# RWKV recurrence and gated feed-forward on one core: START worked out anew, VectorE's and GpSimd's shares exchanged

## The chip, the cores and the metric

One core of a Trainium2 chip. Five engines work side by side: TensorE (matmul and weight load), VectorE, ScalarE, GpSimd and SyncE, which issues most DMAs. The metric is the device time of one execution in microseconds; lower is better. SBUF is the on-chip memory of 128 partitions, PSUM the accumulator memory that TensorE writes. GpSimd's operands here all lie in SBUF.

## What is computed

A linear recurrence over 768 steps for 4 sequences of 8 heads with 48 channels, and on its result a feed-forward layer of 384 to 1536 to 384 channels for all 3072 tokens:

```
for t in range(S):                                   # r, k, v: (4, 8, 768, 48); w, u: (8, 48)
    cur = einsum('bhd,bhe->bhde', u[None] * kt, vt)
    y[:, :, t] = einsum('bhd,bhde->bhe', rt, state + cur)
    state = w[None, :, :, None] * state + einsum('bhd,bhe->bhde', kt, vt)
x = y as (3072, 384)
out = (1 / (1 + exp(-(x @ w_gate))) * (x @ w_val)) @ w_out
```

## The kernel before, in words

**Attention.** The steps are cut into 12 chunks of 64 tokens, and each chunk into two groups of heads: 24 groups, GROUPS[n] = (chunk, half), the half with index 1 first. For one group: loads of the channel layout (L, 512 KB) and the token layout (X, 400 KB); VectorE or GpSimd multiplies queries (R or Rv, line 303), keys (k, line 309) and token keys (T or Tv, line 313) by powers of w; ScalarE makes the keys with u (A, line 282); TensorE makes the 64 x 64 scores (Z, line 350); VectorE copies them through the masks into a score tile (K, line 364); TensorE applies state and scores (I: from_state, then the scores times v) and makes the outer products of the state's update (O, line 405, through into_y at line 322). ScalarE decays the state (d), VectorE adds to it (s; for chunk 0 a copy, sa, on ScalarE). The result y goes from PSUM to x as a rounded high part (h, ScalarE, line 458) and the low rest (l, VectorE, line 462). Channels of the fourth head pair are moved into free partitions of the other three by small DMAs (fills: F, line 466).

**Feed-forward.** x comes in tiles of two chunks, 512 columns. A matmul is done as three passes over high and low parts, low weights first. The hidden channels lie in 12 blocks f. Per block: 18 matmuls up into two PSUM banks (U, line 499), sigmoid of one (g, ScalarE, line 508), product (m, VectorE, line 512), high part (H, ScalarE, line 517), low part (q on GpSimd, qv on VectorE, line 521), 9 matmuls down into three accumulators (D, line 537). For tile 0 blocks 0 and 1 are done for each chunk by itself, with 256 columns: items 0 and 1 are chunk 0, items 2 and 3 chunk 1; items 4 to 13 are blocks 2 to 11 with 512.

**Weights** arrive as 64-bit floats, 1152 KB a block (W, line 232), and are turned into two 32-bit parts in the kernel: ScalarE scales the upper words (c, line 238), VectorE joins (j: three operations, lines 244 to 246), ScalarE rounds the high part (w, line 252), GpSimd (o) or VectorE (ov) takes the low part (line 255). Block 0 is done in halves (c0, j0, w0, o0, o0v).

**Order.** Nothing is scheduled by the compiler: every engine runs its instructions in the order in which the code issues them. START is a list of steps, written out, that covers the attention of chunks 0 to 3 (groups 0 to 7) and the whole feed-forward of tile 0 with the weights of all blocks; the number behind the dot is the group, the block (W, c, j, w, o) or the item (U, g, m, H, q, D). After it a regular loop does tiles 1 to 5 with attention in fixed slots. What sets the order around START is, besides that list, which buffers are free: three of `chan`, three of `toks`, two of `dec`, and three PSUM banks called `ring`, of which each U and each I takes two. A step that finds its buffer in use waits, and with it all that is queued behind it on its engine, SyncE's DMAs too. Other names in START: tk, ti, tp are VectorE's tables of powers, tc constants (GpSimd) with ScalarE's table load, tt a turn of the table on TensorE, tn its copy by ScalarE.

Of the kernel before, what the change touches and what calls it, by code (L numbers as in the profile page):

```python
# [17 lines left out]
B, H, S, D = 4, 8, 768, 48  # L18
# [6 lines left out]
CT = B * C  # L25
# [13 lines left out]


START = """
tk ti tp L.0 Rv.0 W.0 tc A.0 k.0 c0.0 tt L.1 c0.1 X.0 Z.0 j0.0 tn K.0 X.3 I.0 A.1 Tv.0 w0.0 X.1 h.0
k.1 R.1 Z.1 j0.1 l.0 L.2 R.2 K.1 A.2 L.3 k.2 O.0 sa.0 T.1 w0.1 I.1 h.1 Rv.3 W.1 l.1 c.1 Z.2 K.2 L.4
o0.1 O.1 sa.1 o0.0 j.1 F.0 U.0 A.3 W.2 X.2 k.3 g.0 w.1 I.2 m.0 H.0 Tv.2 O.2 ov.1 d.2 X.7 R.4 h.2 s.2
l.2 A.4 Z.3 U.1 K.3 k.4 g.1 T.3 L.5 m.1 c.2 I.3 j.2 d.3 O.3 Z.4 h.3 H.1 W.4 q.0 X.4 D.0 w.2 l.3 s.3
W.7 F.2 c.4 K.4 W.3 U.2 g.2 q.1 A.5 m.2 Rv.5 k.5 T.4 U.3 g.3 L.6 X.5 o.2 j.4 I.4 d.4 H.2 O.4 Z.5 D.1
s.4 q.2 X.6 h.4 W.5 W.6 m.3 l.4 D.2 Tv.5 c.3 j.3 w.4 A.6 H.3 U.4 K.5 g.4 w.3 I.5 m.4 L.7 ov.3 q.3 O.5
d.5 W.10 R.6 h.5 H.4 ov.4 l.5 s.5 q.4 c.5 D.3 k.6 c.6 U.5 g.5 D.4 A.7 W.9 W.8 j.5 w.5 m.5 H.5 U.6 j.6
w.6 k.7 g.6 q.5 D.5 ov.5 Z.6 m.6 U.7 ov.6 c.8 H.6 c.7 K.6 g.7 q.6 Tv.6 I.6 O.6 Rv.7 Z.7 m.7 H.7 D.6
d.6 q.7 D.7 j.7 h.6 w.7 l.6 s.6 ov.7 j.8 U.8 g.8 w.8 m.8 K.7 H.8 qv.8 ov.8 c.9 U.9 g.9 c.10 j.9 D.8  # L50
m.9 U.10 w.9 F.6 ov.9 g.10 m.10 H.9 I.7 H.10 qv.9 qv.10 W.11 c.11 d.7 T.7 O.7 D.9 j.10 h.7 w.10 s.7
l.7 D.10 ov.10 j.11 U.11 g.11 m.11 H.11 qv.11 U.12 w.11 ov.11 D.11 g.12 m.12 F.7 H.12 qv.12 U.13 g.13
D.12 m.13 H.13 q.13
"""


# [1 line left out]
def rwkv_then_moe(ctx: ExitStack, tc: tile.TileContext, wd, ch, tk, rt, ut, wt, rk0, vn0, wd0, out):  # L58
    nc = tc.nc
# [21 lines left out]
    def one_bank():  # L81
        return ring.tile([P, 512], F32, name="ring")
# [12 lines left out]
    w = wu[:, 0]  # L95
# [162 lines left out]
    xt, dec, ga, yb, kv = {}, {}, {}, {}, {}  # L258
# [135 lines left out]

    def outer(n, banks=None):
        k, v = toks[n][:, 0], toks[n][:, 1]
        if banks is not None:
            kv[n] = banks
        for p, p2 in PP:
            for be in range(2):  # L400
                for gm in range(2):
                    row, at = slice(64 * gm, 64 * gm + 64), (4 * p + 2 * (be ^ gm) + p2) * D
                    m, o = D if be else 64, 256 + (2 * p + p2) * D
                    if banks is not None:
                        nc.tensor.matmul(  # L405
                            banks[64 * be : 64 * be + m, gm ^ be, o - 256 : o - 256 + D],
                            k[row, at : at + m], v[row, at : at + D], start=True, stop=True,
                        )
# [20 lines left out]
    def add_state(n, copy=nc.vector.tensor_copy):  # L429
        g, st = states(n)  # L430
        for s in range(2):
            y = (kv[n][:, s, 0 : 4 * D] if n in kv else yb[n][s][:, 256 : 256 + 4 * D])[0:112]
            y = y.rearrange("q (p x) -> q p x", p=2)
            if GROUPS[n][0]:
                nc.vector.tensor_tensor(st[:, :, s], st[:, :, s], y, ALU.add)
            else:
                copy(out=st[:, :, s], in_=y)
# [105 lines left out]
    def accumulators():  # L543
        return [pacc.tile([P, 512], F32, name=f"acc{d}") for d in range(3)]
# [77 lines left out]
    n = FIRST  # L622
# [51 lines left out]
    with tc.If(bad != 0):  # L674
        with ExitStack() as g:
# [65 lines left out]
            x = xp.tile([P, 3, 2, 512], F32R, name="xgr", tag="xt")  # L741
            with tc.For_i(0, NC, 2) as c:
# [11 lines left out]
                m = Moe(x, accumulators(), slice(0, 512))  # L754
# [103 lines left out]
```

## Time and profile before

| | |
|---|---|
| median of 3 runs | 532.45 us (531.23 to 532.75) |
| the profiled execution's own time | 534.04 us |
| its span, first to last instruction | 532.1 us |
| TensorE busy | 510.8 us, 5232 matmuls |
| VectorE busy | 217.9 us |
| ScalarE busy | 171.7 us |
| GpSimd busy | 174.3 us |
| moved by DMA | 48.03 MB |

START ends near 121 us. TensorE's busy time counts matmuls that are pipelined, so a busy TensorE is not TensorE at its peak: 18 matmuls of 256 columns take 4.21 us in one place and 2.42 in another. Idle time of the other engines costs nothing by itself.

### The profile page before, as it was taken

The numbers are of one execution on the slowest core, as the hardware profiler recorded it, in microseconds if no ns is written. First come the engines' busy times: TensorE is split into PE (matmuls) and PEld (weight loads), VectorE is DVE, ScalarE is ACT, GpSimd is POOL, SyncE is SP. The second block draws the span as 40 slices with busy tenths as digits, with TensorE's granted clock in tenths as the row PEclk, the third lists the DMA queues.
The fourth block names the chain that finished last, engine by engine and source line by source line (L and its number), as shares of the span: only waits on it lengthen the run. The fifth ranks groups of instructions, "written<-read, shape, count | busy, mean of one in ns | idle before, by whom it ended". The sixth has DMA issues, their size and how long they took to land.

```text
span 532.1 us, 11993 instructions
## 1 busy us (share of the span) xinstructions
PE 510.8 (96%) x5232; PEld 425.2 (80%) x5232; DVE 217.9 (41%) x379; ACT 171.7 (32%) x358; POOL 174.3 (33%) x156
## 2 busy tenths in 40 slices
PE   3779999999999999999999999999999999999995
PEld 3769878888888888888888888888888888888884
DVE  7798999962333432422414413314414311111111
ACT  5576754532123222331322322313322212221211
POOL 3343332002815555145145154253342311111120
PEclk9998999999999999999999999999999999999998
DMA  8786903063022124311303402113400001100001
GB/s 319 296 294 255 413 4 100 1 221 126 6 87 87 30 77 132 109 48 40 96 3 105 147 0 87 48 48 107 145 1 17 9 5 20 61 0 1 0 1 63
DMA packets 15562, 48.03 MB, mean 90 GB/s; under 512 B 2352, under 2 KB 4784, under 8 KB 14096
## 3 DMA queue, kind: packets, MB, share of 16 engines
q1 hardware_dynamic: 15360, 46.94, 25.6%
q8 instruction: 43, 0.70, 0.6%
q10 hardware_dynamic: 144, 0.26, 0.1%
q14 instruction: 15, 0.12, 0.1%
HBM read 40.12 MB, written 4.72 MB: 84 GB/s over the span
## 4 chain that ended last, share of the span: by engine, by line
PE 90%; DMA 5%; DVE 3%; ACT 1%; issue 1%; SPq 0%; DVEq 0%
PE ring L499 54%; PE acc L537 28%; PE ring L322 4%; PE sc L350 2%; DMA chan<-in_ch 1%; DMA toks<-in_tk 1%; DMA xt<-xt 1%; PE sc L405 1%; DMA wr<-in_wt 1%; DVE wf L245 1%; DVE score L364 1%; DVE wf L246 1%; DVE wx L255 0%; ACT wf L238 0%; DVE wf L244 0%
## 5 line engine op out<-in xcount | busy, mean ns | idle before, releaser
L499 PE MATMUL ring<-xt,wx 128*128 128x512 f32 (+1 forms) x1332 | 309.7, 387 | 2.3 <-DMA xt<-xt 1.8
L499 PEld LDWEIGHTS ring<-xt,wx 128*128 128x128 f32 x1332 | 248.3, 191 | 51.6 <-ACT wx L252 2.0
L521 POOL TENSOR_TENSOR h<-sg,h 128x512 fp32r<-128x512 f32 (+1 forms) x68 | 90.8, 1336 | 324.9 <-ACT h L517 324.9
L537 PE MATMUL acc<-h,wx 128*128 128x512 f32 (+1 forms) x666 | 161.4, 388 | 0.0
L512 DVE TENSOR_TENSOR sg<-ring,sg 128x512 f32<-128x512 f32 (+1 forms) x74 | 50.0, 676 | 264.8 <-PE ring L499 264.7
L537 PEld LDWEIGHTS acc<-h,wx 128*128 128x128 f32 x666 | 121.2, 188 | 25.2 <-DVE h L521 0.2
L508 ACT ACTIVATE sg<-ring 128x512 f32<-128x512 f32 (+1 forms) x74 | 43.3, 585 | 177.1 <-PE ring L499 177.1
L517 ACT CAST h<-sg 128x512 fp32r<-128x512 f32 (+1 forms) x74 | 45.2, 611 | 106.3 <-DVE sg L512 106.3
L424 ACT ACTIVATE state<-state,every 112x96 f32<-112x96 f32 x80 | 23.6, 365 | 25.8 <-PE ring L322 25.8
L462 DVE TENSOR_TENSOR xt<-ring,xt 112x256 fp32r<-112x256 f32 (+1 forms) x52 | 19.9, 418 | 27.8 <-ACT xt L458 27.7
L303 POOL TENSOR_TENSOR dec<-chan,every 128x512 f32<-128x512 f32 x20 | 24.0, 1201 | 14.2 <-PE ring L322 6.2
L364 DVE COPY_PREDICATED score<-masks,sc 128x512 f32<-128x512 int32 x32 | 23.6, 739 | 1.0
L458 ACT CAST xt<-ring 112x256 fp32r<-112x256 f32 (+1 forms) x52 | 17.1, 373 | 17.3 <-PE ring L322 16.0
L322 PE MATMUL ring<-score,toks 64*64 64x64 f32 (+1 forms) x768 | 18.6, 229 | 3.8 <-DVE score L364 2.0
L313 POOL TENSOR_TENSOR toks<-toks,tabn 128x384 f32<-128x384 f32 x18 | 19.6, 1090 | 0.0
L322 PEld LDWEIGHTS ring<-score,toks 64*48 64x48 f32 (+1 forms) x768 | 15.3, 133 | 5.0 <-POOL dec L303 1.9
L252 ACT CAST wx<-wf 128x1152 fp32r<-128x1152 f32 (+1 forms) x13 | 14.0, 1080 | 14.9 <-DVE wf L246 14.9
L246 DVE SCALAR_TENSOR_TENSOR wf<-wr,wf 128x1152 int32<-128x1152 int32 (+1 forms) x13 | 18.4, 1415 | 0.5
L322 PEld LDWEIGHTS ring<-dec,state 48*48 48x48 f32 (+1 forms) x704 | 12.0, 127 | 7.2 <-issue 6.6
L350 PE MATMUL sc<-dec,chan 48*64 48x64 f32 x768 | 17.6, 231 | 0.1
L289 POOL TENSOR_TENSOR dec<-dec,ub 128x384 f32<-128x384 f32 x16 | 16.7, 1043 | 0.0
L291 POOL TENSOR_TENSOR dec<-dec,toks 128x384 f32<-128x384 f32 x16 | 16.3, 1018 | 1.3
(56 smaller groups left out, 236.3 us busy)
## 6 DMA issues: line engine op xcount, KB each, us to landing
wr<-in_wt SPq DMA_DIRECT2D x11, 1152.0 KB, 9.3
chan<-in_ch SPq DMA_DIRECT2D x24, 512.0 KB, 4.7
toks<-in_tk SPq DMA_DIRECT2D x24, 400.0 KB, 4.7
out_y<-wf SPq DMA_DIRECT2D x17, 256.0 KB, 2.3
dec<-in_rt SPq DMA_DIRECT2D x16, 192.0 KB, 2.6
xt<-xt SPq DMA_DIRECT2D x30, 64.0 KB, 2.3
wr<-in_wt SPq DMA_DIRECT2D x2, 576.0 KB
xt<-xt SPq DMA_DIRECT2D x12, 32.0 KB, 5.2
```

Of the source, the lines that this page charges most:

```text
L246: nc.vector.scalar_tensor_tensor(g, low, 29, g, ALU.logical_shift_right, ALU.bitwise_or)
L303: eng.tensor_tensor(v4(t[:, 0]), v4(chan[n][:, 0]), bc2(table_of(n)), ALU.mult)
L322: nc.tensor.matmul(yb[n][bank][64 * half : 64 * half + m, cs], lhsT, rhs, start=first, stop=stop, skip_group_check=True,)
L350: nc.tensor.matmul(sc[64 * gm : 64 * gm + 64, be ^ gm, o : o + C], kk[row, cs : cs + C], rr[row, cs : cs + C], start=True, stop=True,)
L364: nc.vector.copy_predicated(t.rearrange("q (b m i) -> q b m i", b=2, m=4), masks[:, m].bitcast(I32).unsqueeze(1).unsqueeze(1).broadcast_to ...
L424: nc.scalar.activation(st[:, p, s], st[:, p, s], AF.Copy, scale=pw[0:112, 4 * g + 2 * p + s, 64:65],)
L499: nc.tensor.matmul(o[:, self.cols], w[a][:, g * DM + kt * P : g * DM + (kt + 1) * P], self.x[:, kt, b, self.cols], start=(k == 0), stop=(k ...
L508: nc.scalar.activation(sg[:, c], self.pair[f][0][:, c], AF.Sigmoid)
L512: nc.vector.tensor_tensor(sg[:, c], self.pair.pop(f)[1][:, c], sg[:, c], ALU.mult)
L517: nc.scalar.copy(out=h[:, 0, c], in_=sg[:, c])
L521: eng.tensor_tensor(h[:, 1, c], self.sg.pop(f)[:, c], h[:, 0, c], ALU.subtract)
L537: nc.tensor.matmul(self.acc[d][:, self.cols], w[a][:, 2 * DM + d * P : 2 * DM + (d + 1) * P], h[:, b, self.cols], start=(f == 0 and k == 0 ...
```

## The change

START is another order of the same 267 steps, with some of them on another engine:

- from GpSimd to VectorE: R.1, one half of o0 (o0.1), q.4, q.5, q.7
- from VectorE to GpSimd: R.7; T.2, T.5, T.6; the low weights of blocks 1, 7 and 9; q.11
- T.7 goes from GpSimd to VectorE, so that VectorE has 21 steps of the kinds R, T, o and q, one of them a half, where it had 23
- the first steps of TensorE are Z.0, tt, O.0, I.0, Z.1, O.1, I.1 in place of tt, Z.0, I.0, Z.1, O.0, I.1, Z.2, O.1; D.1 stands ahead of U.2
- W.1 is loaded before all tokens, j0.1 follows j0.0, and j.1 is made before l.0
- the fills are issued half by SyncE and half by ScalarE for groups 0, 6 and 7 (G in place of F)
- O may come before I: the PSUM banks of y are taken by whichever comes first (y_of)

```
@@ START @@
-tk ti tp L.0 Rv.0 W.0 tc A.0 k.0 c0.0 tt L.1 c0.1 X.0 Z.0 j0.0 tn K.0 X.3 I.0 A.1 Tv.0 w0.0 X.1 h.0
-k.1 R.1 Z.1 j0.1 l.0 L.2 R.2 K.1 A.2 L.3 k.2 O.0 sa.0 T.1 w0.1 I.1 h.1 Rv.3 W.1 l.1 c.1 Z.2 K.2 L.4
-o0.1 O.1 sa.1 o0.0 j.1 F.0 U.0 A.3 W.2 X.2 k.3 g.0 w.1 I.2 m.0 H.0 Tv.2 O.2 ov.1 d.2 X.7 R.4 h.2 s.2
-l.2 A.4 Z.3 U.1 K.3 k.4 g.1 T.3 L.5 m.1 c.2 I.3 j.2 d.3 O.3 Z.4 h.3 H.1 W.4 q.0 X.4 D.0 w.2 l.3 s.3
-W.7 F.2 c.4 K.4 W.3 U.2 g.2 q.1 A.5 m.2 Rv.5 k.5 T.4 U.3 g.3 L.6 X.5 o.2 j.4 I.4 d.4 H.2 O.4 Z.5 D.1
-s.4 q.2 X.6 h.4 W.5 W.6 m.3 l.4 D.2 Tv.5 c.3 j.3 w.4 A.6 H.3 U.4 K.5 g.4 w.3 I.5 m.4 L.7 ov.3 q.3 O.5
-d.5 W.10 R.6 h.5 H.4 ov.4 l.5 s.5 q.4 c.5 D.3 k.6 c.6 U.5 g.5 D.4 A.7 W.9 W.8 j.5 w.5 m.5 H.5 U.6 j.6
-w.6 k.7 g.6 q.5 D.5 ov.5 Z.6 m.6 U.7 ov.6 c.8 H.6 c.7 K.6 g.7 q.6 Tv.6 I.6 O.6 Rv.7 Z.7 m.7 H.7 D.6
-d.6 q.7 D.7 j.7 h.6 w.7 l.6 s.6 ov.7 j.8 U.8 g.8 w.8 m.8 K.7 H.8 qv.8 ov.8 c.9 U.9 g.9 c.10 j.9 D.8
-m.9 U.10 w.9 F.6 ov.9 g.10 m.10 H.9 I.7 H.10 qv.9 qv.10 W.11 c.11 d.7 T.7 O.7 D.9 j.10 h.7 w.10 s.7
-l.7 D.10 ov.10 j.11 U.11 g.11 m.11 H.11 qv.11 U.12 w.11 ov.11 D.11 g.12 m.12 F.7 H.12 qv.12 U.13 g.13
-D.12 m.13 H.13 q.13
+L.0 tk ti A.0 tp Rv.0 W.0 k.0 c0.0 j0.0 c0.1 j0.1 L.1 A.1 tc k.1 Z.0 K.0 w0.0 o0.0 tt W.1 X.0 tn Tv.0
+c.1 w0.1 O.0 Rv.1 X.2 sa.0 I.0 L.2 A.2 L.3 X.1 W.2 h.0 X.4 Z.1 j.1 l.0 G.0 K.1 T.1 O.1 k.2 o0v.1 w.1 I.1
+h.1 R.2 Rv.3 sa.1 l.1 A.3 Z.2 X.3 L.5 K.2 o.1 k.3 T.2 c.2 j.2 U.0 g.0 m.0 I.2 Z.3 L.4 d.2 h.2 O.2 s.2
+w.2 l.2 H.0 K.3 U.1 g.1 R.4 m.1 A.4 k.4 T.3 q.0 W.3 I.3 Rv.5 O.3 H.1 h.3 l.3 T.4 Z.4 q.1 d.3 c.3 K.4 D.0
+D.1 L.7 A.5 s.3 F.2 U.2 g.2 o.2 U.3 g.3 W.4 c.4 X.6 j.3 m.2 H.2 X.5 I.4 d.4 k.5 m.3 O.4 Z.5 h.4 j.4 w.3
+H.3 s.4 L.6 l.4 w.4 q.2 D.2 X.7 K.5 ov.4 R.6 q.3 W.6 U.4 ov.3 g.4 I.5 m.4 d.5 h.5 l.5 T.5 c.6 W.5 O.5
+R.7 W.7 D.3 s.5 A.7 j.6 H.4 c.5 qv.4 U.5 g.5 m.5 k.7 A.6 j.5 U.6 H.5 w.6 w.5 qv.5 k.6 D.4 D.5 g.6 ov.5
+m.6 c.7 Z.6 K.6 T.6 W.8 j.7 U.7 H.6 q.6 g.7 I.6 h.6 w.7 ov.6 o.7 W.10 d.6 l.6 O.6 Z.7 c.8 s.6 D.6 c.10
+m.7 j.8 W.11 H.7 W.9 qv.7 U.8 g.8 m.8 w.8 K.7 Tv.7 ov.8 H.8 qv.8 U.9 g.9 m.9 D.7 c.9 j.9 H.9 qv.9 U.10
+g.10 I.7 O.7 w.9 o.9 m.10 G.6 D.8 h.7 l.7 d.7 s.7 j.10 H.10 qv.10 c.11 U.11 w.10 ov.10 D.9 g.11 U.12
+m.11 H.11 G.7 q.11 j.11 w.11 D.10 ov.11 D.11 g.12 m.12 H.12 U.13 qv.12 g.13 m.13 D.12 H.13 q.13

+    def y_of(n):
+        if n not in yb:
+            yb[n] = one_bank(), one_bank()
+        return yb[n]
...
-            yb[n][bank][64 * half : 64 * half + m, cs], lhsT, rhs,
+            y_of(n)[bank][64 * half : 64 * half + m, cs], lhsT, rhs,
...
-        yb[n] = one_bank(), one_bank()
+        y_of(n)
...
-    def fill(x, j, cols):
-        for lo, to in ((0, 48), (64, 112)):
-            nc.sync.dma_start(
+    def fill(x, j, cols, queues):
+        for (lo, to), queue in zip(((0, 48), (64, 112)), queues):
+            queue.dma_start(
...
-    def fills(n):
+    def fills(n, queues=(nc.sync, nc.sync)):
...
+        "G": lambda n: fills(n, (nc.sync, nc.scalar)),
```

## Rows read from the trace of the kernel before

**Rows 1.** The page, part 1: busy time, share of the span, instructions.

```profile
PE 510.8 (96%) x5232; PEld 425.2 (80%) x5232; DVE 217.9 (41%) x379; ACT 171.7 (32%) x358; POOL 174.3 (33%) x156
```

**Rows 2.** Waits of TensorE from 58 us on: releaser, total, times, longest.

```profile
PE ring L322 <- DVE sg L512: 0.3, 1, 0.3
```

**Rows 3.** Waits of TensorE up to 60 us.

```profile
PE ring L322 <- issue: 2.2, 2, 2.0
PE ring L322 <- DVE score L364: 2.0, 2, 1.7
PE ring L499 <- DMA xt<-xt: 1.8, 1, 1.8
```

**Rows 4.** Windows: length, busy time by engine, PEclk, DMA share, GB/s.

```profile
5.00:17.00 12.00, 7.62 (x221) 6.77 (x221) 11.62 (x21) 6.96 (x19) 3.42 (x3) 1.00 1.02 412
...
42.00:43.00 1.00, 1.00 (x7) 1.00 (x6) 0.74 (x1) 0.61 (x3) 1.00 (x1) 0.50 0.98 409
```

**Rows 5.** The chain in order of time: start, length, what.

```profile
59.22 4.11 PE ring L499 x18
...
114.89 4.08 PE ring L499 x18
```

**Rows 6.** Timeline up to U.0: start, length, engine, line, operation.

```profile
5.03 1.28 ACT L282 ACTIVATE dec<-chan,wu 128x128 f32<-128x128 f32 x4 [2.78 <-DMA chan<-in_ch]
...
6.56 0.68 DVE L309 TENSOR_TENSOR chan<-chan,every 128x512 f32<-128x512 f32 x1
...
13.82 0.75 DVE L462 TENSOR_TENSOR xt<-ring,xt 112x256 fp32r<-112x256 f32 x2
...
14.66 4.62 SPq L466 DMA_DIRECT2D xt<-xt  x6
...
23.39 4.21 PE L499 MATMUL ring<-xt,wx 128*128 128x256 f32 x18
```

**Rows 7.** Groups by line and shape: busy us, mean ns, idle before.

```profile
L521 POOL TENSOR_TENSOR h<-sg,h 128x512 fp32r<-128x512 f32 x64 | 84.9, 1327 | 309.5 <-ACT h L517 309.5
...
L303 POOL TENSOR_TENSOR dec<-chan,every 128x512 f32<-128x512 f32 x20 | 24.0, 1201 | 14.2 <-PE ring L322 6.2 <-DVE wf L246 4.9 <-DMA chan<-in_ch 3.1
L364 DVE COPY_PREDICATED score<-masks,sc 128x512 f32<-128x512 int32 x32 | 23.6, 739 | 1.0
...
L313 POOL TENSOR_TENSOR toks<-toks,tabn 128x384 f32<-128x384 f32 x18 | 19.6, 1090 | 0.0
...
L245 DVE SCALAR_TENSOR_TENSOR wf<-wr,wf 128x1152 int32<-128x1152 int32 x11 | 15.0, 1359 | 0.4
...
L244 DVE TENSOR_SCALAR wf<-wf 128x1152 int32<-128x1152 int32 x11 | 8.3, 752 | 0.2 <-ACT wf L238 0.2
...
L255 POOL TENSOR_TENSOR wx<-wf,wx 128x1152 fp32r<-128x1152 f32 x1 | 2.7, 2669 | 0.0
```

**Rows 8.** Timeline from 28 to 42 us.

```profile
29.93 2.16 DVE L255 TENSOR_TENSOR wx<-wf,wx 128x1152 fp32r<-128x1152 f32 x1
...
32.14 2.42 PE L499 MATMUL ring<-xt,wx 128*128 128x256 f32 x18 [0.47 <-DVE wx L255]
...
40.49 6.10 PE L499 MATMUL ring<-xt,wx 128*128 128x256 f32 x36 [1.79 <-DMA xt<-xt]
...
40.73 0.62 DVE L435 TENSOR_TENSOR state<-state,ring 112x192 f32<-112x192 f32 x2
```

**Rows 9.** Timeline of VectorE and GpSimd from 65 to 76 us.

```profile
66.73 1.97 POOL L521 TENSOR_TENSOR h<-sg,h 128x512 fp32r<-128x512 f32 x1 [5.92 <-ACT h L517]
67.59 2.33 DVE L246 SCALAR_TENSOR_TENSOR wf<-wr,wf 128x1152 int32<-128x1152 int32 x1
70.44 1.34 DVE L255 TENSOR_TENSOR wx<-wf,wx 128x1152 fp32r<-128x1152 f32 x1
73.58 1.52 DVE L364 COPY_PREDICATED score<-masks,sc 128x512 f32<-128x512 int32 x2
73.70 1.31 POOL L521 TENSOR_TENSOR h<-sg,h 128x512 fp32r<-128x512 f32 x1 [5.00 <-ACT h L517]
```

More of the change, by code (lines that the diff above doesn't have):

```diff
@@ L476, in fills @@
             for j in range(3) if g == 1 else ():
-                fill(xt[ti], j, slice(co, co + CT))
+                fill(xt[ti], j, slice(co, co + CT), queues)
         elif c == TILES[ti][-1]:
             for j in (2,) if g == 1 else (0, 1):
-                fill(xt[ti], j, slice(0, 2 * CT))
+                fill(xt[ti], j, slice(0, 2 * CT), queues)
     PASS = ((1, 0), (0, 0), (0, 1))
@@ L586, in rwkv_then_moe @@
         "k": keys, "T": token_keys, "Z": scores, "K": keep, "I": apply, "O": outer,
-        "d": decay_state, "s": add_state, "sa": lambda n: add_state(n, nc.scalar.copy), "h": x_high, "l": x_low, "F": fills, "D": finish,
+        "d": decay_state, "s": add_state, "sa": lambda n: add_state(n, nc.scalar.copy), "h": x_high, "l": x_low, "F": fills, "G": lambda n: fills(n, (nc.sync, nc.scalar)), "D": finish,
         "tc": constants, "tk": channel_table, "ti": inverses, "tp": token_powers,
```

## The prediction, made before the changed kernel ran

> **What bounds the kernel now.** I read the page first. TensorE is busy for 510.8 us, 96% of the span, and VectorE for 217.9 [rows 1]. So I asked in the view of waits who keeps TensorE waiting, and when. From 58 us to the end nothing does for longer than 0.3 us [rows 2]: from there TensorE is the bound, and a new order can only win by bringing it to the same amount of work earlier. Up to 58 us it waits for its own issue, with no releaser in the profile (2.2 us), for VectorE's score copy (2.0) and for the fill of the second chunk's x (1.8) [rows 3]. The view of windows shows what feeds that start: from 5 to 17 us the DMA rings are full, at a share of 1.02 and 412 GB/s, and VectorE is busy for 11.62 us of the 12. After the fill TensorE also ran at half its granted clock, the lower of its levels (1.2 of 2.4 GHz): 0.50 at 42 to 43 us [rows 4]. The chain, read last, gives the checkpoints: U.5 starts at 59.22 and U.13, the last one of START, at 114.89 [rows 5].
>
> So I walk the new order engine by engine, each step with its duration from before, and compare five checkpoints. The diff permutes START's steps: none is added or lost. TensorE has the same 52 steps in nearly the same order, so a checkpoint's time compares directly, but for a D step that passed it.
>
> **Up to U.0: 0.7 us lost.** The DMA order puts W.1 (1.18 MB) ahead of all tokens. L.0 lands at 5.0 (A.0 starts on it) [rows 6]. Behind it until X.0 lie W.0, L.1, W.1 and X.0, 3.29 MB, at 412 GB/s 8.0 us: X.0 lands at 13.1, X.1 about 17.7, W.2 about 20.6. VectorE is done with k.0 at 7.2, then takes both halves of j.0 (2.0 each), k.1 (0.7) and the score copy K.0 (1.5) [rows 6, 7]: 13.5. Tv.0 waits there for GpSimd's o0.0 and ends at 14.7. Then O.0 and I.0, 32 small matmuls each, 1.1 us each at the early pace, which is half the later one (U.0's 18 matmuls take 4.21 us, U.1's 2.42 [rows 6, 8]), so that h.0 ends near 17.6; VectorE meanwhile does Rv.1 and j.1 (3.5), so l.0 ends at 19.6, where it ended at 14.6 [rows 6]. This is the loss of five microseconds that the order accepts, and two edits give it back. The six fill DMAs took SP 4.62 us to issue [rows 6]; as G.0 three go to each of SP and ScalarE, 2.3 us. And W.1 is already joined. U.0 starts at 24.1 against 23.39 [rows 6]. ScalarE pays: it stands at G.0 until l.0 ends and then for 2.3 us, and w.1, h.1 (thus l.1), sa.1 and A.3 are queued behind it. I count that in all that follows. A TensorE code wait like the 2.0 us one of before falls into the wait for T.1 here; uncovered, it costs up to 0.8 us more.
>
> Edits at nothing: taking TensorE's bank at O rather than I (the bank is free); Z.0 ahead of the turn matmuls (tn is needed only when X.0 lands); ScalarE's table load behind A.1, where tn would wait for up to 1.3 us and ends at 13.2, just as X.0 lands; if X.0 came sooner it would cost that.
>
> **Up to U.1: 0.6 us lost.** l.1 waits for h.1 and ends at 25.0, K.2 1.5, k.3 0.7; j.2 starts with c.2 at 27.7. It is now ahead of m.0, and GpSimd's R.4, released by I.2's first half at 29.0, takes its turn inside it: 3.5 and 1.2 [rows 7], to 32.3. m.0 ends at 32.7 and frees the bank of U.1: 32.7 against 32.14 [rows 8]; TensorE stands idle from O.2's end at 31.2 on. What is saved is that o.1 sits on GpSimd, under l.1 and K.2, which read PSUM; before, ov.1 took 2.16 us on VectorE [rows 8], where ov.5 takes 1.34 [rows 9], because GpSimd was at work beside it.
>
> **Up to U.3's end: 2.7 us won.** s.2, l.2, K.3, m.1, k.4, Rv.5, l.3, K.4, s.3 run without a j between them; before, j.2 (3.5) stood ahead of l.3 and s.3, which frees U.2's second bank. s.3 ends at 40.5 against 41.35 [rows 8]. F.2 is issued behind l.2 from 34.1 to 37.6 on empty rings and lands by 39. Both D.0 and D.1 fit in ahead of U.2 (D.1 was behind U.3), so U.2 follows at 40.2 without the idle 1.8 us. U.2 and U.3 took 6.10 us at the dropped clock; two of U.1's length, 2.42, are 4.84 [rows 8]. U.3 ends at 44.9 against 46.6 (40.49 and 6.10) with one more D of half size (1.0) done: 1.7 + 1.0.
>
> **Up to U.5: 2.3 us won.** Rv.1 and the half o0.1 are added to VectorE and Tv.2, Tv.5 and ov.1 leave it. j.3, j.4, s.4, l.4, K.5, ov.4, ov.3, m.4 follow in turn; of GpSimd's q.2, q.3, R.6, T.5 and R.7 I count 0.65 us inside j.4 and 1.2 between ov.4 and ov.3. m.4 ends at 56.9 and U.5 starts there: 59.2 - 56.9 [rows 5].
>
> **Up to U.13: 2.3 us won.** VectorE's steps from j.6 to ov.11 sum to 45.4 us (seven j at 3.46, two operations of 1.36 and one of 0.75 [rows 7]; five ov at 1.27, six qv and seven m at 0.6, two K at 1.43, l, s, k and Tv 4.1 together, each from start to start, with 0.08 of overlap), one q.6 of 1.05 inside j.7, and waits for TensorE and ScalarE of some 6.5. From s.5 at 58.2 that puts ov.11's end at 111.2, 1.4 us before TensorE, walked with its own steps, wants it at 112.6. 114.9 - 112.6 = 2.3; I round to 2.2. The profiled execution lies 1.9 us above its span, and 1.6 above the median; the sum is a difference, so it comes off the median: 532.45 - 2.2 = 530.25.
>
> **Turns on SBUF.** The price of a GpSimd step under VectorE decides. q.5 started at 66.73 and took 1.97 us; the VectorE operation that started at 67.59, the last of j.6, took 2.33 where its like takes 1.36. q.6 started under K.6, which reads PSUM, and neither lengthened: 1.31 and 1.52 [rows 9]. So a GpSimd operation costs VectorE its own length if it meets one whose inputs are both in SBUF, nothing else. The Trainium skill says the same (SBUF — State Buffer, Who interferes with whom: the shared port pair is an exclusive lock, and a VectorE operation with two SBUF inputs contends with a GpSimd one that reads SBUF); the rows agree. It also speaks against the change (Perfetto Trace Analysis, Optimizing Scalar/DVE Operations: moving work between these two might not help): taken to the letter every moved operation costs its length, and the sum comes out at the third rival's 536.7; by the rows it is 530.25.
>
> **Rivals.** (1) Forecast, 530.25, chance 0.42: between 529.3 and 531.2.
> (2) More, 528.4, chance 0.12: what I count as late at U.0 and U.1 stays covered (0.7) and VectorE's two turns before U.5 (1.85) miss it. For it: q.2, q.3 and R.7 are short against the PSUM steps around them. Against: every such step of the walk must fit.
> (3) Slower, 536.7, chance 0.2: GpSimd's turns bind VectorE. Five steps, T.6, q.6, o.7, o.9 and q.11, take 1.0, 1.3, 2.7, 2.7 and 1.3, 9.0 us, in 57 to 112 us [rows 7]; I count 1.05. If all fall on two-operand steps VectorE is 7.9 us later, ov.11 at 119.1 and U.13 with it: 4.2 after 114.9. It decides from 3.7 us of the 7.9 on: 1.4 of slack and 2.3 of gain. For it: nearly four fifths of VectorE's time there is in j, ov and qv. Against: o.7 and o.9 become free just as l.6, s.6, m.7 and m.10, l.7 run.
> (4) No change, 532.4, chance 0.26: the half clock, which followed 1.8 us of idle time, follows the 1.5 us before U.1 instead (1.3 us back), with the uncovered code wait (0.8). For it: TensorE's start has more holes than before.
>
> A measurement of this kernel tells about 0.3%, 1.6 us, from no change. Faster by more than that means below 530.85: most of the forecast (0.36 of 0.42) and all of the second, 0.48. Same: the rest of the forecast and most of the fourth, 0.27. Slower: the third and a little of the fourth, 0.25. For eight in ten, from 527.8 (the second with its half microsecond of noise) to 535.3, which leaves out the upper half of the third. The forecast's own range is 529.3 to 531.2.
>
> **What will show it.** U.0 starts near 24, U.1 near 32.7, U.3 ends near 45 with D.1 behind it, U.5 starts near 57 and U.13 near 112.6. l.0 ends near 19.6. The column of granted clock stays at 1.00 from 41 to 45. VectorE's share from 58 to 112 rises but its j keep 3.5 us, save one. I am wrong if U.0 comes after 26, if j.2 ends after 34, if TensorE waits for VectorE after 58 us for more than a microsecond in all, or if ov.11 is what U.13 waits for.

## The result and the profile after

The changed kernel took 538.96 us (median of 6 runs, 537.85 to 541.16) against 532.60 (6 runs, 531.23 to 533.88) for the kernel before. Over the pairs that is a ratio of 1.0125, with a 95% interval of 1.0103 to 1.0146: 6.7 us slower, where I had forecast 2.2 us faster and a range that ended at 535.3. The profiled execution took 538.82 us, with a span of 537.0 against 532.1; the rows below explain these 4.9 us, not all of the 6.7.

The page, part 1, of the changed kernel (busy time, share of the span, instructions):

```profile
PE 509.5 (95%) x5232; PEld 423.3 (79%) x5232; DVE 213.7 (40%) x377; ACT 173.1 (32%) x359; POOL 177.3 (33%) x158
```

TensorE's busy time is no longer than before [rows 1], so the time is in its waits. The view of TensorE's waits (releaser, total, times, longest), first up to 58 us, then from there to the end:

```profile
PE sc L354 <- DVE chan L308: 8.7, 1, 8.7
PE ring L326 <- DVE toks L312: 3.5, 1, 3.5
PE ring L503 <- DVE xt L466: 1.7, 2, 1.3
PE ring L503 <- ACT xt L462: 1.3, 1, 1.3
PE ring L326 <- issue: 1.2, 3, 0.8
...
PE ring L326 <- DVE xt L466: 2.1, 2, 1.0
```

Against [rows 2, 3] four things are new: the first scores wait until 8.7 us; O.0 waits 3.5 us for Tv.0; U.0 waits twice, for the high and for the low part of x (L462, L466); and in the stretch that had no wait above 0.3 us there are two of 1.05 us for the low part of x. The 1.8 us for the fill is gone, and so is the half clock at 42 to 43 us, as the view of windows shows:

```profile
5.00:17.00 12.00, 4.25 (x134) 3.90 (x138) 10.32 (x18) 9.97 (x21) 1.53 (x1) 1.00 1.03 421
42.00:43.00 1.00, 1.00 (x10) 1.00 (x10) 0.97 (x2) 1.00 (x2) 0.35 (x1) 1.00 0.47 157
```

The rings are as full as before in the first stretch [rows 4], but VectorE is busy for 10.32 us of the 12 instead of 11.62. The chain gives the two late checkpoints (start, length, what):

```profile
62.09 8.19 PE ring L503 x36
...
119.36 4.08 PE ring L503 x18
```

U.5 starts 2.9 us later than in [rows 5], U.13 4.5 us later. The timeline up to U.0, row by row against [rows 6]:

```profile
5.35 1.28 ACT L281 ACT_TABLE_LOAD   x1 [5.35 <-DMA chan<-in_ch]
6.65 1.28 ACT L281 ACTIVATE dec<-chan,wu 128x128 f32<-128x128 f32 x4
7.96 0.69 DVE L308 TENSOR_TENSOR chan<-chan,every 128x512 f32<-128x512 f32 x1 [1.44 <-ACT dec L281]
13.09 1.50 DVE L368 COPY_PREDICATED score<-masks,sc 128x512 f32<-128x512 int32 x2
14.49 0.54 DVE L312 TENSOR_TENSOR toks<-toks,tabn 128x384 f32<-128x384 f32 x1
19.01 0.75 DVE L466 TENSOR_TENSOR xt<-ring,xt 112x256 fp32r<-112x256 f32 x2
19.79 3.09 ACTq L470 DMA_DIRECT2D xt<-xt  x3
22.92 1.15 ACT L251 CAST wx<-wf 128x1152 fp32r<-128x1152 f32 x1 [4.19 <-DVE wx L254]
23.98 1.50 ACT L462 CAST xt<-ring 48x256 fp32r<-48x256 f32 x4
25.50 0.54 ACT L441 COPY state<-ring 112x192 f32<-112x192 f32 x2
25.53 0.80 PE L503 MATMUL ring<-xt,wx 128*128 128x256 f32 x2 [1.30 <-ACT xt L462]
25.85 1.73 DVE L466 TENSOR_TENSOR xt<-ring,xt 48x256 fp32r<-48x256 f32 x4 [2.66 <-ACT state L441]
27.63 3.78 PE L503 MATMUL ring<-xt,wx 128*128 128x256 f32 x16 [1.31 <-DVE xt L466]
```

These are, in order: ScalarE's table load behind its wait for L.0, A.0, k.0, K.0, Tv.0, l.0, ScalarE's half of the fills, w.1, h.1, sa.1, two matmuls of U.0, l.1, and the other 16. Against the walk the time goes between l.0, which ends on time, and l.1. There l.1 has two delays. One is that h.1 starts late, at 23.98. The other is sa.1, the copy of the state out of the same two PSUM banks that l.1 reads: the new list puts it ahead of l.1, the old one behind, and l.1's releaser is now sa.1. The rows of h.1 and l.1 before:

```profile
19.80 1.51 ACT L458 CAST xt<-ring 48x256 fp32r<-48x256 f32 x4 [0.45 <-PE ring L322]
20.57 1.75 DVE L462 TENSOR_TENSOR xt<-ring,xt 48x256 fp32r<-48x256 f32 x4 [3.41 <-ACT xt L458]
```

There l.1 started 0.77 us behind h.1's start, in the changed kernel 1.87. The runs below agree wherever VectorE stood free for l.1: 0.77 or 0.78 us in e6, e8, e9, f1, f4 and s1, where sa.1 is behind l.1, and 1.87 or 1.88 in e1, e3, e4, e5, e7, f5, f8 and s2, where it is ahead. So sa.1's place is 1.1 us of the late l.1. No run moves it by itself, so what it costs the kernel in the end isn't measured.

The second place, the stretch around O.5:

```profile
58.17 0.68 PE L326 MATMUL ring<-score,toks 64*64 64x64 f32 x32 [0.29 <-issue]
58.93 0.65 ACT L462 CAST xt<-ring 112x256 fp32r<-112x256 f32 x2
59.33 0.76 DVE L466 TENSOR_TENSOR xt<-ring,xt 112x256 fp32r<-112x256 f32 x2 [1.09 <-ACT xt L462]
59.90 0.90 PE L326 MATMUL ring<-toks 64*64 64x48 f32 x32 [1.05 <-DVE xt L466]
```

I.5 (58.17) writes y; h.5 and l.5 read it; only then does O.5 (59.90) run. O writes columns 256 and up of the two PSUM banks whose columns 0 to 255 are y. It needs nothing of h or l, but it stands behind them in the list, and a write into a bank waits for the reads of that bank that were issued before it. The Trainium skill (PSUM — Partial Sum Buffer, PSUM bank collisions raise a hardware error) says why the code must order them: writer and reader are to be kept apart by bank, not by address. The trace agrees, with 1.05 us here and at O.6. Before, O.6 stood ahead of h.6, and O.5 ahead of h.5.

### The profile page after: what moved, and what is told of

Its sections match the earlier page's. It is cut to its first block, busy times and chain, and to the rows that moved or that the text cites. A ratio compares the mean times of both kernels' runs of the same rounds, so it can differ in the third digit from the quotient of the medians.

```text
span 537.0 us, 11993 instructions
## 1 busy us (share of the span) xinstructions
PE 509.5 (95%) x5232; PEld 423.3 (79%) x5232; DVE 213.7 (40%) x377; ACT 173.1 (32%) x359; POOL 177.3 (33%) x158
## 4 chain that ended last, share of the span: by engine, by line
PE 90%; DVE 4%; ACT 2%; issue 1%; DMA 1%; ACTq 1%; SPq 0%; DVEq 0%
PE ring L503 54%; PE acc L541 28%; PE ring L326 5%; PE sc L354 2%; PE sc L409 1%; DVE xt L466 1%; DVE wf L244 1%; DMA chan<-in_ch 1%; DVE score L368 1%; ACT xt L462 1%; ACTq L470 1%; DVE wf L245 1%; DVE wf L243 0%; ACT wx L251 0%; DVE chan L308 0%
## 5 line engine op out<-in xcount | busy, mean ns | idle before, releaser
L525 POOL TENSOR_TENSOR h<-sg,h 128x512 fp32r<-128x512 f32 (+1 forms) x66 | 84.8, 1284 | 297.5 <-ACT h L521 297.5
L512 ACT ACTIVATE sg<-ring 128x512 f32<-128x512 f32 (+1 forms) x74 | 43.5, 587 | 179.2 <-PE ring L503 179.2
L466 DVE TENSOR_TENSOR xt<-ring,xt 112x256 fp32r<-112x256 f32 (+1 forms) x52 | 20.0, 420 | 30.8 <-ACT xt L462 28.0
L302 POOL TENSOR_TENSOR dec<-chan,every 128x512 f32<-128x512 f32 x20 | 25.9, 1293 | 9.5 <-PE ring L326 7.4
L462 ACT CAST xt<-ring 112x256 fp32r<-112x256 f32 (+1 forms) x52 | 17.2, 374 | 20.7 <-PE ring L326 20.4
L254 POOL TENSOR_TENSOR wx<-wf,wx 128x1152 fp32r<-128x1152 f32 (+1 forms) x5 | 12.1, 2429 | 32.2 <-ACT wx L251 32.2
L354 PEld LDWEIGHTS sc<-dec,chan 48*64 48x64 f32 x768 | 15.1, 145 | 9.5 <-DVE chan L308 8.7
```

The costliest lines, as they stand in the source:

```text
L302: eng.tensor_tensor(v4(t[:, 0]), v4(chan[n][:, 0]), bc2(table_of(n)), ALU.mult)
L354: nc.tensor.matmul(sc[64 * gm : 64 * gm + 64, be ^ gm, o : o + C], kk[row, cs : cs + C], rr[row, cs : cs + C], start=True, stop=True,)
L512: nc.scalar.activation(sg[:, c], self.pair[f][0][:, c], AF.Sigmoid)
L525: eng.tensor_tensor(h[:, 1, c], self.sg.pop(f)[:, c], h[:, 0, c], ALU.subtract)
```

## The experiments

Theory 1: the loss is three placements (ScalarE's table load and its queue ahead of h.1, and the O steps behind h and l). Theory 2: GpSimd's turns on SBUF, my third rival. Ratios are to the kernel before on the same chip, with their 95% interval; its medians there were 532.75 to 533.57. In the diffs "..." stands for steps that are as they were.

**e1, the table load first.**

```
-L.0 tk ti A.0 ... A.1 tc k.1
+L.0 tk ti tc A.0 ... A.1 k.1
```

> The changed kernel with one step moved: tc, and with it ScalarE's table load for the sigmoid, ahead of A.0. Theory 1 (the loss is made of three waits: a late table load on ScalarE, the fills that ScalarE issues ahead of h.1, and O steps that stand behind h and l in the list and so wait for their reads of the same PSUM banks): one table load falls under the first transfer, A.0 starts at about 5.2 instead of 6.65, k.0 at 6.5 instead of 7.96, and all up to U.0 comes 1.4 us earlier; 537.6 against 539.0. If the fills are what l.1 waits for, part of it is lost again and the gain may fall to 1.0. Theory 2 (GpSimd's turns on SBUF hold VectorE up all along, as the third rival of the prediction has it): the early 1.4 us is not what sets the end; within 0.5 us of 539.0.

538.91 us, 1.0104 [1.0055, 1.0152]: no gain to be seen. k.0 did come 1.3 us earlier, at 6.64, but k.1 then met a GpSimd step. Timeline:

```profile
11.28 1.45 POOL L254 TENSOR_TENSOR wx<-wf,wx 128x576 fp32r<-128x576 f32 x1 [6.77 <-ACT wx L251]
11.39 1.89 DVE L308 TENSOR_TENSOR chan<-chan,every 128x512 f32<-128x512 f32 x1
13.20 1.48 DVE L368 COPY_PREDICATED score<-masks,sc 128x512 f32<-128x512 int32 x2
```

k.1 took 1.89 us where the changed kernel's took 0.68, and K.0 started at 13.20 instead of 13.09. The earlier start was given back whole by the time K.0 started.

**e2, the first fills on SyncE alone.** G.0 becomes F.0 in the changed kernel.

> The changed kernel with G.0 as F.0: all six fills of group 0 issued by SyncE. Theory 1: ScalarE no longer stands at the issue from 19.8 to 22.9; w.1 runs from 19.1, h.1 starts when I.1 ends (22.5, was 23.98), l.1 ends near 25 instead of 27.58. The sixth fill lands near 26 instead of 23.96, so U.0 runs on from 26 instead of 27.63: 1.6 us won, 537.4; the X.3, L.5, L.4 behind the fills on SyncE come 2 us later, which may take some of it. Theory 2: nothing changes, 539.0, or a little slower for the later loads.

541.69 us, 1.0146 [1.0101, 1.0191]. w.1 came 4 us earlier and released GpSimd's o.1 into VectorE's work:

```profile
21.19 3.08 POOL L254 TENSOR_TENSOR wx<-wf,wx 128x1152 fp32r<-128x1152 f32 x1
21.71 3.18 DVE L254 TENSOR_TENSOR wx<-wf,wx 128x576 fp32r<-128x576 f32 x1
```

o0v.1, the second row, takes 0.75 us in the changed kernel. l.1 started at 26.22, no earlier than at 25.85, and U.0's sixteen started at 27.99. A miss for the single edit, for the same reason as e1.

**e3, the O steps ahead of what reads their banks.**

```
-sa.0 I.0 ... d.2 h.2 O.2 ... d.5 h.5 l.5 T.5 c.6 W.5 O.5 ... I.6 h.6 w.7 ov.6 o.7 W.10 d.6 l.6 O.6
+I.0 sa.0 ... O.2 d.2 h.2 ... T.5 O.5 d.5 h.5 l.5 c.6 W.5 ... I.6 O.6 h.6 w.7 ov.6 o.7 W.10 d.6 l.6
```

> The changed kernel with four steps moved in the list only, no engine's own order changed but for the place of sa.0: O.2, O.5 and O.6 (and T.5, which O.5 needs) stand ahead of d, h and l of their group, and sa.0 behind I.0. TensorE's order is the same. Theory 1: O.5 and O.6 no longer wait for l.5 and l.6 (1.05 us each in the profile after, in the stretch where TensorE is the bound), O.2 not for h.2, and I.0 not for sa.0 (0.5): the two waits of 1.05 go, 2.1 us won, with some of the rest up to 2.6: 536.6. Theory 2: TensorE waits for VectorE anyway, the waits move to the next U: 538.5 to 539.

535.77 us, 1.0048 [1.0032, 1.0064], an interval clear of the changed kernel's 1.0103 to 1.0146. TensorE's waits from 58 us to the end, and the chain:

```profile
PE ring L326 <- issue: 0.6, 2, 0.3
```

```profile
60.19 8.19 PE ring L503 x36
...
116.12 4.08 PE ring L503 x18
```

Both waits of 1.05 us are gone. U.13 starts 3.24 us earlier than in the changed kernel (119.36): 2.1 are the waits, 0.84 is a stop at 49.78 without a releaser that didn't come here, and that this is due to the edit isn't shown. By the ratios the edit gives back more than half of the loss. It is the simplest of the edits, but the two waits alone are only a third of the loss, and the rest of its gain isn't itemised.

**e4, the late shares given back to VectorE:** T.6, o.7, o.9 and q.11 become Tv.6, ov.7, ov.9 and qv.11, in place.

> The changed kernel with four GpSimd steps given back to VectorE at their places: o.7, o.9, T.6, q.11 as ov.7, ov.9, Tv.6, qv.11 (7.7 us of GpSimd's time off, 4.0 us of VectorE's on). Theory 1: none of the four met VectorE at a cost but q.11 (1.0 in j.11), and VectorE has waits of 0.7 to 1.6 us there: within 1.0 us of 539.0, rather slower. Theory 2: VectorE is freed of up to 7.7 us of turns for 4.0 us of work; 2 to 4 us faster, 535 to 537.

544.73 us, 1.0208 [1.0162, 1.0254]: the opposite of what theory 2 says, and more than the microsecond that theory 1 allowed. The timeline shows a longer wait:

```profile
83.82 1.36 DVE L254 TENSOR_TENSOR wx<-wf,wx 128x1152 fp32r<-128x1152 f32 x1 [0.90 <-ACT wx L251]
85.10 0.75 DVE L466 TENSOR_TENSOR xt<-ring,xt 112x256 fp32r<-112x256 f32 x2
85.57 0.69 PE L326 MATMUL ring<-toks 64*64 64x48 f32 x6 [3.55 <-DVE xt L466]
```

ov.7 now stands ahead of l.6, so l.6 is late and O.6 waits for 3.55 us; behind it the granted clock fell (window, the seventh number):

```profile
85.00:88.00 3.00, 2.43 (x85) 2.39 (x88) 1.72 (x6) 2.12 (x2) 0.00 (x0) 0.50 0.13 22
```

So e4 is no clean test of the shares: it measures O.6's place once more. The timeline of the changed kernel is the better one. T.6 and o.9 lengthened no VectorE operation, o.7 one of j.8 by 0.35 us (the first row, 0.75 elsewhere), q.11 one of j.11 by 0.97 (the second, 1.36 elsewhere):

```profile
85.35 1.10 DVE L243 TENSOR_SCALAR wf<-wf 128x1152 int32<-128x1152 int32 x1 [0.22 <-ACT wf L237]
...
113.55 2.33 DVE L245 SCALAR_TENSOR_TENSOR wf<-wr,wf 128x1152 int32<-128x1152 int32 x1
```

No U waits behind 58 us in the changed kernel, so these late shares are not its loss.

**e6, the mechanism put into the kernel before:** O.5 moved from ahead of d.5 to behind l.5.

> The kernel before with one step moved in its list, O.5 from ahead of h.5 to behind l.5, the order of no engine changed. Theory 1 (an O that stands behind h and l of its group in the list must wait for their reads of its PSUM banks): TensorE stands still from I.5's end (57.2) until l.5 ends (60.3), 3 us, and its clock may fall after that for one to two more; 535.5 to 537.5 against 532.7. If the order in the list among different engines did not matter, no change.

537.55 us, 1.0069 [1.0041, 1.0096]. Waits of TensorE up to 62 us:

```profile
PE ring L321 <- DVE xt L461: 3.1, 2, 2.8
```

The wait appears with the one edit, 2.75 us at 56.10, and the granted clock was at 0.50 for 3.4 us behind it. So this placement makes O.5 wait, in either order.

**e5 and e7, repairs on top of e3.** e5: F.0 for G.0, and w.1 behind sa.1. e7: e5 with I.0 ahead of O.0 and I.1 ahead of O.1. Neither moves sa.1.

> The changed kernel with the O steps moved as in the third run, G.0 as F.0 (all on SyncE) and w.1 behind sa.1 on ScalarE, so that neither stands ahead of h.1 and o.1 can not meet the half o0v.1 as it did in the second run. Theory 1 (U.0 needs l.1, l.1 needs h.1, and h.1 stood behind G.0 and w.1): h.1 starts at 22.5, l.1 ends near 25.2 instead of 27.4, U.0 runs on from about 26, when the last fill lands: 1.4 us better than the third run's 535.8, so 534.4. If the order of j.1 and the tokens is what holds it, nothing: 535.8.

> The fifth run's companion (O steps moved, fills on SyncE, w.1 late) with the outer products put back behind the inner ones for groups 0 and 1: I.0 ahead of O.0, I.1 ahead of O.1. If the outer products first are what makes the start late, h.0 and h.1 come 1.1 us sooner each and U.0 starts at about 25 instead of 26.07: 1 us better than that run. If VectorE's j.1, which stands ahead of l.0, is what l.0 waits for, and K.1 what I.1 waits for, U.0 starts at 26 as there: no difference, 535.2 to 536.

e5: 535.71 us, 1.0050 [1.0032, 1.0068], no better than e3. l.1 did start 1.6 us earlier than in the changed kernel (24.29). In the profiled execution TensorE then stood for 1.12 us at 49.23 with no releaser, and the clock fell behind that until 57 us:

```profile
50.00:51.00 1.00, 0.66 (x25) 0.66 (x29) 0.96 (x2) 0.21 (x1) 0.27 (x1) 0.62 0.00 0
51.00:52.00 1.00, 1.00 (x49) 1.00 (x46) 1.00 (x2) 1.00 (x3) 1.00 (x1) 0.50 0.28 45
```

But that execution took 538.86 us, the longest of twelve, so these rows don't explain the median: why the earlier l.1 brought nothing there stays open.

e7: 537.59 us, 1.0090 [1.0069, 1.0112]: worse than e5, with two stops without a releaser, 2.74 and 1.69 us, at 17.7 and 20.8 us.

**f1, f3, f4: single ingredients in the kernel before.** f1 moves W.1 ahead of X.0; f3 makes F.0 a G.0 right behind l.0; f4 puts O.0 ahead of I.0 (behind Tv.0) and O.1 ahead of I.1.

> The kernel before with one edit: the 1.18 MB of W.1 are loaded ahead of X.0, as the change does. Theory 1 (the early loss is the order of the DMAs: what U.0 needs comes behind weights that it doesn't need): X.0 lands some 2.9 us later (1.18 MB at 412 GB/s), near 13, l.1 follows at 24 to 25 where it ended at 22.3, U.0 starts 1 to 2 us later: 533.5 to 534.5 us. Rival (the early loss is in the order of the engines, the DMAs have slack): within 0.6 us of before.

> The kernel before with one edit: the first fills are issued half by SyncE and half by ScalarE, behind l.0 in the list, as the change does. Theory 1 (ScalarE pays for three issues with its own queue): SyncE is done 2.3 us earlier, but A.2, Z.2 and h.1 come 2.4 to 3.1 us later on ScalarE, l.1 near 24.5, U.0 1 us later: 533 to 534.5 us. Rival (the fills are the limit of U.0): U.0 a microsecond earlier, 531.5.

> The kernel before with one edit: O.0 ahead of I.0 and O.1 ahead of I.1. Theory 1: O.0 takes 1.1 us of TensorE ahead of I.0 and its Tv.0 is ready by 11.4, so h.0 and l.0 move by 1 to 1.5 us and h.1 by about as much, of which l.1 passes 0.5 to 1 us on to U.0: 532.8 to 533.8 us. Rival (the outer products have a hole to lie in): within 0.5 us of before.

f1: 535.45 us, 1.0033 [1.0018, 1.0049], 1.8 us slower, as theory 1 had it, and U.0 started 1.5 us later (24.93). Tv.0 started at 13.42, where it started at 10.81 before, and waited for its tokens:

```profile
13.42 0.56 DVE L312 TENSOR_TENSOR toks<-toks,tabn 128x384 f32<-128x384 f32 x1 [2.26 <-DMA toks<-in_tk]
```

How the late U.0 reaches the end isn't shown. In the profiled execution, 533.93 us and under its median, the clock stayed at 1.00 from 40 to 45 us and U.13 started at 114.21, 0.7 us earlier than in [rows 5].

f4: 533.82 us, 1.0007 [0.9989, 1.0026]: the order of the outer products cost nothing that can be measured. f3: 538.89 us, 1.0104 [1.0081, 1.0128], far more than either side expected, but it doesn't answer its question: placed right behind l.0 the fills also passed L.2, L.3, W.1 and L.4 in SyncE's queue, and A.2 waited 8.12 us for L.2, which the changed kernel issues ahead of the fills. What the split alone costs stays open.

**f5, f7, f8: the changed start repaired**, all with the O steps of e3. f5: X.0 and X.1 ahead of W.1, block 1's c, j and w later, F.0, I.1 ahead of O.1. f7: the table load first, K.0 behind j0.0 alone, X.0 ahead of W.1, l.0 ahead of j.1 (which stays ahead of l.1), F.0, w.1 behind l.1. f8: f7 with l.1 ahead of j.1 and m.0 ahead of j.2. In all three sa.1 stays ahead of l.1.

> The changed kernel with the O steps moved as before, the first fills on SyncE alone, I.1 ahead of O.1, and the tokens X.0 and X.1 ahead of W.1, so that c.1, j.1 and w.1 go behind l.0, l.1's inputs and sa.1. Theory 1 (the early loss is the order of the DMAs): X.0 lands near 10.5, l.0 ends at 15 to 16.5, l.1 at 21 to 22.5, U.0 starts at 23 to 24.5 and the time is 531.5 to 533.5 us. Rival (weights block 1 is then late, as U.1 needs o.1): U.1 waits for o.1 by 1 to 2 us, and with an idle of that length the granted clock falls once: 535 to 537 us.

> The changed kernel with the O steps moved and its start put right in one go: the table load first, K.0 behind j0.0 alone, X.0 ahead of W.1, l.0 ahead of j.1 (which stands ahead of l.1), the first fills on SyncE, w.1 behind l.1; everything from A.3 on as in the changed kernel. Theory 1 (what is left of the loss is the late l.1): Tv.0 ends near 11.4 (15.0 in the changed kernel), l.0 near 15.5, l.1 at 22 to 24, U.0 starts at 23 to 24.5, and with 1 to 2.3 us less at U.0 the time is 533.3 to 534.8, where the O steps alone left 535.8. Rival (the start is covered; TensorE's holes and the half clock behind them decide): U.0 comes as early, but U.1 or I.2 wait for what is late next, and the time stays at 535 to 537.

> As the run before, with j.1 behind K.2, not ahead of l.1, and j.2 behind m.0. Theory 1: l.1 ends 1 to 2 us earlier still, at 21 to 22, U.0 at 22 to 23; o.1 is ready by 31 and U.1 starts at 32 to 33: 532 to 534. Rival: U.1 waits for o.1 or K.3 for j.2, 535 to 537.

f5: 542.79 us, 1.0173 [1.0143, 1.0204]; f7: 536.51, 1.0070 [1.0055, 1.0085]; f8: 539.62, 1.0124 [1.0106, 1.0142]. All miss theory 1; f7 lies where its rival had it. In f5 Tv.0 starts when it did in the changed kernel:

```profile
14.37 0.54 DVE L312 TENSOR_TENSOR toks<-toks,tabn 128x384 f32<-128x384 f32 x1
```

VectorE is at work without a pause from 7.85 to 15.5 us there, so it is its own list (j0.0, j0.1 and k.1 ahead of K.0) and not the tokens that sets Tv.0. Then I.2 waited 3.87 us for g.0, which stood behind w.1 and c.2 on ScalarE. f7 cleared that list, and GpSimd's o0.0 fell on Tv.0, its T.2, R.4 and T.3 on j.2:

```profile
11.56 1.43 DVE L313 TENSOR_TENSOR toks<-toks,tabn 128x384 f32<-128x384 f32 x1 [0.80 <-ACT tabn L203]
...
32.28 2.28 DVE L245 SCALAR_TENSOR_TENSOR wf<-wr,wf 128x1152 int32<-128x1152 int32 x1
34.60 2.03 DVE L246 SCALAR_TENSOR_TENSOR wf<-wr,wf 128x1152 int32<-128x1152 int32 x1
```

l.1 started at 26.16, right behind j.1 and no earlier than in the changed kernel; j.2 took 5.9 us instead of 3.5, and U.1 waited 2.82 us for the m.0 behind it. f8's l.1 started at 24.29, and then I.2 waited 4.09 us for g.0.

**s1, s2, e8, e9: the two orders mixed.** s1 is the start of before up to F.0 with the rest of the changed order (O moved), s2 the changed start up to U.0 with the rest of before. e8 is before with j.2 behind c.4, thus behind l.3 and s.3, w.2 behind A.5, and W.7 behind F.2 and W.3, which is what was to let U.3 end earlier in the changed order; e9 is e8 with W.7 left in its place.

> The order of before up to F.0 (the shares of before in it), and behind it the rest of the changed order, with O.2, O.5 and O.6 ahead of h of their group. Theory 1 (the loss lies in what stands ahead of U.0, and in the O steps behind h and l; the rest of the new order is as good as the old or better): U.0 runs from about 23.5 as in before, and the rest gives the 1.0 us or so by which the changed kernel with the O steps moved caught up between U.0 (3.7 late) and the end (2.6 to 3.0 late); 531.5 to 532.3 beside 532.7 for before. Theory 2 (the shares in the rest cost as well): 533.5 or more.

> The mirror image: the changed order up to what stands ahead of U.0, and behind it the rest of the order of before, with its shares and its O steps ahead of h. Theory 1: U.0 ends near 31.3, 3.7 us later than in before, and nothing behind it gives that back, save the 1.7 us of lowered clock at 41 to 45 if TensorE is not idle there: 535 to 536.5. Theory 2: the start alone costs little, under 1.5 us: 533 to 534.

> The kernel before with what the changed order did well ahead of U.2: j.2 (with w.2 and c.4 around it) behind l.3 and s.3 instead of ahead of them, and W.7 behind F.2 and W.3 instead of ahead of them. l.3 ends near 38.6 instead of 40.7, s.3 near 39.2 instead of 41.35, the last fill lands by 39.2 instead of 41.2, U.2 starts near 39.2 instead of 40.5, without 1.8 us of idle time ahead of it; if the clock then does not fall (1.7 us at 41 to 45 in before), 3 us won: 529.7. If only the idle time goes and the clock falls all the same, 531.4. If j.2's delay makes U.4 wait for o.2, nothing is won: 532.7.

> The kernel before with the first half of that edit alone: j.2, w.2 and c.4 moved, W.7 left ahead of F.2. The last fills still land behind W.7, near 41, so U.2 waits as before and the clock falls as before: 532.2 to 532.7. If VectorE alone had set U.2, 530 to 531 as with both.

s1: 539.21 us, 1.0114 [1.0087, 1.0142]; s2: 539.59, 1.0126 [1.0101, 1.0151]; e8: 536.86, 1.0072 [1.0050, 1.0094]; e9: 536.64, 1.0067 [1.0048, 1.0086]. s1 lies on the side of its theory 2; s2, e8 and e9 are slower than anything that I had expected of them. In s1 U.0 ended at 27.1 us, 4 us earlier than in the changed kernel, yet the order behind it is made for the other start: I.2 waited 3.53 us for g.0 and U.1 1.76 for the m.0 behind j.2, and the granted clock was at 0.50 from about 30 to 43.5 us. In s2 TensorE waited 2.57 us for K.4 ahead of U.2. e8 brought U.3's end from 46.6 to 41.7 us and lost it in the next two steps (waits of TensorE, 28 to 60 us):

```profile
PE ring L321 <- DVE sg L511: 2.3, 2, 2.0
PE sc L349 <- DVE chan L308: 2.0, 1, 2.0
```

The first is m.2, behind j.2 and K.4; the second k.5, behind an Rv.5 that met o.2 and took 2.87 us instead of 0.68. No version that I ran beats the kernel before; f4 can't be told from it.

## Why the prediction was wrong

The checkpoints in the profiled executions, in us:

| | before | forecast | changed | e3 |
|---|---|---|---|---|
| U.0 starts: two matmuls, the other 16 | 23.39 | 24.1 | 25.53, 27.63 | 25.30, 27.41 |
| U.1 starts | 32.14 | 32.7 | 34.27 | 34.76 |
| U.3 ends | 46.59, D.1 still to come | 44.9 | 47.31 | 47.73 |
| U.5 starts | 59.22 | 56.9 | 62.09 | 60.19 |
| U.13 starts | 114.89 | 112.6 | 119.36 | 116.12 |

Against the forecast U.13 is 6.8 us late: 2.4 by U.3's end, 2.8 more by U.5, 1.6 more by U.13. Against before it is 4.5 late, and all of that comes behind U.3: at U.3's end the changed kernel is some 0.5 us ahead, if D.1, which it has done by then, counts 1.2 (an estimate: D.0 and D.1 together took 2.41), though before had by then lost 1.7 us to the half clock at 41 to 45 (an estimate from its mean of 0.57 there).

**Up to U.0: this step failed.** X.0 landed by 13.2, forecast 13.1, and l.0 ended at 19.76 us, forecast 19.6. The second is in part luck: h.0 came 1.1 us late, which doesn't show because l.0 stood behind j.1 anyway. But I let U.0 start at 24.1, with l.1 waiting for h.1 alone and ending at 25.0. U.0 is groups 0 and 1: its first two matmuls need h.1, the third needs l.1. l.1 ended at 27.58, 2.6 us later than my walk, and 16 of U.0's 18 matmuls started then. Of the 2.6 us, 1.5 are ScalarE's queue, which I charged with too little: its three issues took 3.09 us instead of my 2.3, and w.1 (1.15 us) stood between them and h.1, which could have gone when I.1 ended at 22.5 and went at 23.98. The other 1.1 are sa.1, which I put ahead of l.1 at nothing. The table load, which I had placed at tc, sat behind A.0's wait for L.0 (1.28 us), with a second one at tc (10.77); k.0 ended at 8.65 us where my walk had 7.2, and the turn that I had put down for Tv.0, and that didn't come, made most of that up. Of the ingredients, weights first is worth 1.8 us by itself (f1) and outer products first nothing (f4). That the late l.1 is what e3 leaves, 0.48% or 2.6 us, isn't shown: f5, f7 and f8 were to show it and didn't, and in the profiles e3 stands level with before at U.3's end (by the same estimate) and falls back behind it.

**Up to U.1 and U.3: carried on, with 0.8 us more.** j.2 ended at 33.14 (forecast 32.3). R.4's turn, which I had counted inside it, fell the other way: j.2 took its 3.5 us, and R.4 beside it 1.96 where its like takes 1.20 [rows 7]. The fill no longer delays U.2, the clock stayed at 1.00, and D.1 stood ahead: the mechanism held. s.3 ended at 43.95 and not at 40.5, since U.1's second half and with it all behind it came later.

**Up to U.5 and U.13: this step failed too.** I put O.5 and O.6 behind h and l of their group at nothing. The only price that I gave a move of O was that of the PSUM bank that it takes, "the bank is free"; the readers that it now follows had none. O.5 and O.6 cost 1.05 us each, in the stretch where TensorE is the bound and nothing gives it back; from U.3's end to U.5 the changed kernel took 14.8 us where I had 12.0, and e3 took 12.5. e3 and e6 show this part: 2.1 us of waits in the changed kernel. The stop of 0.84 us without a releaser lies in the same stretch; what makes up the rest isn't shown.

**The rivals.** The third, GpSimd's turns binding VectorE, is not what happened in the stretch for which I priced it, 57 to 112 us: U.13 doesn't wait for ov.11 (it ended at 118.5, U.13 ran from 119.36), and of the j between them only j.8 (3.8 us) and j.11 (4.5, beside q.11) took longer than 3.5. VectorE's busy time from 58 to 112 us, which I had rising, fell, from 50.7 to 43.6 us. (Of my own 45.4 us there j, ov and qv are 34.2, three quarters and not nearly four fifths.) That a VectorE step can lose what is left of a GpSimd step held in e1, e2, e8 and f7: the rule of the Trainium skill (SBUF — State Buffer, Who interferes with whom) that I set beside my rows agrees with the 1.89 us of k.1. But the turns took away what repairs had gained; they were not the change's loss. The fourth named the half clock: it left 41 to 45 us, and in the changed kernel's profiled execution the column of granted clock reads 1.00 throughout START. So that execution is 4.9 us longer in span though the column shows no loss, while the one of before lost 1.7 us to it. The 0.8 us that I called a code wait is a stop without a releaser in the rows; no run shows its cause. The test that I set, more than a microsecond of waits for VectorE after 58 us, is the one that spoke: 2.1.

## What to carry to other kernels

When a step is moved in a hand-written order, list who reads and writes its buffers around the new place, by whole PSUM bank, and not only whether the buffer is free: a write that needs nothing of its neighbours still waits for the reads that are issued ahead of it (O.5), and here a read by another engine did so too (l.1 behind sa.1). Follow the first consumer of a stage to its last input, through every engine's queue, since a DMA issue or a cast ahead of that input counts whole. And on an engine without slack don't add up the repairs: most of them here released work that met something else.

## What I had not expected of the hardware

- **Short stops cost twice, at times.** Behind stops of 1.1 us (e5, no releaser), 2.75 us (e6) and 3.55 us (e4) the granted clock stood at 0.50, the lower of its levels, for some 3.4 to 7 us, with half of that lost. Behind the two of 1.05 us in the changed kernel's profile it stayed at 1.00; e1's profile has the same two, and the clock fell behind the second (82 to 86 us), e4's has the first, and it fell behind that (59 to 63).
- **The column of granted clock can read 1.00 where TensorE is at the slow pace.** In f4's profile it stood at 0.50 from 18 to 32 us, a loss of 6.8 us by the column, and yet f4 took the time of before. In before it reads 1.00 in that stretch, but U.0's 18 matmuls took 4.21 us there and 4.18 in f4, against 2.42 for U.1's. Up to the end of U.0 the two kernels thus ran at one pace; behind that f4 was slower (I.2's first 32 matmuls took 1.12 us instead of 0.68) and still started U.1 at 32.12, as before did (32.14).
- **The table load moves with the first activation, and can wait with it.** In the changed kernel it ran from 5.35 to 6.63 us, when the L.0 that A.0 waits for was in, though ScalarE was idle before, and a second one of 1.28 us followed at tc. Where tc stands first, in before and in e1, the only one ran from 0.75 us.
- **TensorE's stops without a releaser move with the order:** 2.0 us before [rows 3], 0.8 in the changed kernel, none above 0.9 in e3, 1.1 in e5, 2.7 and 1.7 in e7.
